# A delta-rule attention with two feed-forward layers on one core: a longer tuned order in the attention phase, and 512 columns a product in the gated layer's second part

## The chip, the core and the metric

The kernel runs on one core of a Trainium2 chip. The metric is the device time of one execution in microseconds; the times shown are medians of several runs. The profile is that of one execution, taken by the hardware profiler. TensorE (PE) multiplies matrices into PSUM, VectorE (DVE), ScalarE (ACT) and GpSimd (POOL) do the elementwise work, SyncE (SP) and ScalarE issue the transfers.

## The reference

Three layers, one after the other, all in float32 at their boundaries (the weights come as float64):

```
# attention: 4 batches, 8 heads, 768 steps, 48 dims
k_n = k / (norm(k) + 1e-06)
for t in range(S):
    y[t] = q[t] @ state
    state = state + beta[t] * outer(k_n[t], v[t] - k_n[t] @ state)
x = y as (3072 tokens, 384)
# gated layer: w_gate, w_val (384 x 1536), w_out (1536 x 384)
xn = x / sqrt(mean(x * x) + 1e-06) * rms_g
x = (silu(xn @ w_gate) * (xn @ w_val)) @ w_out
# last layer: w_in (384 x 2048), w_out (2048 x 384)
h = x @ w_in
out = (h * tanh(softplus(h))) @ w_out
```

## The kernel before

**Tiling.** The 768 steps are cut into 12 rows of 64 steps; a row holds 4 x 64 = 256 tokens (T). In the gated layer and the last layer every operand is kept as a high and a low part in float32r (names ending in h and l), and a product is three matmuls: high by high, high by low, low by high. The 1536 inner columns of the gated layer are six pairs of 256 (m); in a pair, f is one half of 128. The tiles of w_gate, w_val and w_out of pair m are `W["g", m]`, `W["v", m]` and `W["o", m]`.

**Stages.** `phase_b1` holds the attention and, between its steps, the first two pairs (FA = 2) of the gated layer for every row (`gated` with `range(FA)`): the partial sums go to `p_d` in HBM, the rows' inputs to `xh_d` and `xl_d`. `phase_b2` runs the other four pairs over all rows, loads the partial sums, adds its own, and so has the input of the last layer; `forms_of` makes the sums and differences of it that the last layer's multiplication scheme wants, splits them and stores them (`xf_d`). `phase_c` is the last layer: triples of transformed products (`triple`) with the products of w_out beside them (`down`, 384 columns). The first triple runs in `between()`, ahead of the last sums of `phase_b2`.

**Order.** All engines execute in the order in which the generators issue. In the attention phase `plan` issues the start by due times (ROW0, ROW1, QP, CV, T, G and so on), and then `merge` weaves a row's stages (listed by name in R2 to R11) with the gated layer (`part_a`), the weight conversions (`cv`) and the next segment's lanes, each by its share. In `phase_b2`, `merge` weaves the gated products (`part_b`) with the conversions, which count 192 in all.

**The second part, row by row.** For each row n and pair m, `gated` computes pg (18 matmuls of 256 columns, two halves of one PSUM tile), the silu into sg on ScalarE, pv (18 matmuls), sg times pv and the high part hh on VectorE, the low part hl on GpSimd. The down products of row n (`down`: 3 outputs x 4 pairs x 6 matmuls = 72) follow after the first pair of row n+1. Each output is then added to y (`finish_b`). Rows are loaded by `load_x` on ScalarE's queue, one row ahead, into a ring of two places (tags xh, xl). The last layer's inputs go into eight tiles `gx` and the same ring (`load_group`).

**Conversions.** `value` turns the float64 bits of 128x384 weights into float32 by one absolute value (ScalarE or VectorE) and four VectorE operations (L270, L273, L278, L281); `prepare_forms` adds and subtracts the w_in blocks (L336); `prepare_rows` does w_out of the last layer.

Of the kernel before, what the change touches and what calls it, by code (L numbers as in the profile page):

```python
# [20 lines left out]
    LN0=0.351,  # L21
    LNT=(103.075, 3.017),
    FAV=[0, 1, 1, 0, 0, 0],
    XDR=[0, 0, 0, 0, 0, 0, 1, 0, 0, 0, 0, 1],
    PDR=[0, 0, 0, 0, 0, 0, 0, 0, 0, 0, 0, 1],
    BLV=[1, 1, 0, 0, 0, 1, 0, 0, 0, 1, 1, 1],
    BAV=[0, 0, 1, 1, 1, 1, 1, 0, 0, 1, 1, 0],
    CB=[12.0, 12.0],
    PF=[5.239, 29.437, 15.946, 7.096, 7.497],
# [6 lines left out]
    LD=2.564,  # L36
# [3 lines left out]
    FP=2,  # L40
    WL=2.0,
# [8 lines left out]
    R1="r nA q0 q1 y v p o0 o1 s0 nB s1 k x0 c0 c1 g".split(),  # L50
    R2="nA r q0 Y nB q1 p y v k o0 o1 c0 c1 g".split(),
    R3="r q0 nA q1 p nB S y T X v Y k c0 o0 c1 g o1".split(),
    R4="nA q0 r T q1 p S y nB X v Y k c0 o0 c1 g o1".split(),
    R5="r nA q0 q1 p S T y nB v X Y o0 c0 k c1 o1 g".split(),
    R6="nA r q0 q1 S T y p X v Y nB k o0 c0 c1 g o1".split(),
    R7="r q0 nA q1 S p T nB v y X Y c0 o0 c1 o1 k g".split(),
    R8="r nA q0 S q1 T p y nB X v Y c1 o0 g c0 k o1".split(),
    R9="r nA q0 q1 S nB T y p X Y c1 c0 v k g o0 o1".split(),
    R10="r q0 q1 S p y X T v o0 Y k o1".split(),
    R11="S r q0 q1 p T v y X Y o0 o1 k".split(),  # L60
    DUE=[-20.443, 5.407, 4.713, 10.95, 10.883, 10.311, 10.883, 10.589, 8.191, 10.779, 10.857, 11.898],
    CVS=[0.353, 25.315, 8.774, -21.306, 9.319, -4.783, 14.063, -23.293, -15.017, -36.281, -27.539, -1.077],
    LR=[-13.795, 25.182, 18.833, 15.016, 19.193, 14.209, 19.088, 16.373, 36.251, 19.526, 57.055, 52.214],
    C={'n': 0.225, 'q': 0.5, 'r': 1.4, 'y': 1.1, 'p': 1.2, 'v': 1.2, 'o': 0.9, 'k': 1.2, 's': 0.172, 'x': 0.45, 'c':
        0.4, 'd': 0.167, 'g': 1.2, 'h': 1.228},
    ROW0=[23.019, 26.819, 30.249, 44.784, 45.626, 49.289, 33.092, 3.864, 53.626, 52.596, 54.116, 59.926, 27.667,
        37.065, 77.944],
    ROW1=[53.942, 41.233, 46.444, 57.746, 50.762, 31.696, 58.427, 60.081, 62.969, 38.184, 36.083, 63.207, 59.815,
        70.152, 81.867, 91.215, 96.339],
    QP=[[37.124, 37.533, 45.096, 22.943, 36.287], [46.104, 51.456, 18.08, 46.719, 54.368], [63.444, 60.96, 65.725,  # L70
        77.666, 71.789], [72.411, 86.727, 78.936, 75.152, 80.107]],
    L=[(19.303, 1.152), (44.964, 1.066)],
    FF=(81.946, 4.733),
    CV=[22.08, 17.591, 24.08, 74.28, 61.944, 44.711, 48.686, 65.195, 50.571, 79.022, 64.689, 83.13, 83.315, 83.796,
# [3 lines left out]
    K1=[4.777, 9.76, -11.197, -13.022],  # L78
    K23=[11.822, 14.842, 13.512, 12.77],
    K4=[45.709, 47.503, 50.123, 37.446],  # L80
    S=[-2.317, 10.764, 23.854, 22.707, 53.127],
    T=[9.259, 12.875, 27.966, 32.334],
    G=[11.277, 15.572, 4.585, 15.695],
    BL=32.701,
    CVN=13.355,
# [115 lines left out]
def kernel(  # L201
# [51 lines left out]
    def prepare(get_pool, key, cut, act=True, low=None, **kw):  # L253
        return [prepare_half(half, get_pool, key, cut, act, low or nc.gpsimd, kw) for half in range(2)]
# [238 lines left out]

    def x_tiles():
        return [xp.tile([128, KD, T], F32R, tag=tag, name=tag, bufs=XB) for tag in ("xh", "xl")]
# [7 lines left out]
    def phase_b1():  # L503
# [34 lines left out]
        bnat = xp.tile([128, KD, T], F32R, tag="xl", name="bnat", bufs=XB).bitcast(F32)  # L538
# [41 lines left out]
        def flat(t):  # L580
            return t.bitcast(F32).rearrange("p a b -> p (a b)")
# [732 lines left out]
        for m in range(FA):  # L1314
            gens.append(prepare(lambda: wa, ("o", m), rows(w_out1, m), act=not P["FAV"][4 + m], low=nc.vector))
# [18 lines left out]
        sq = [xp.tile([128, KD, T], F32R, tag="xh", name="sq", bufs=XB) for _ in range(2)]  # L1334
        sq = [flat(t)[:, 0:16 * D].rearrange("p (u d) -> p u d", d=D) for t in sq]
# [3 lines left out]
        part_a = gated((ps_u, ps_ds, hp, tp), range(FA), range(NR), get_xa, finish_a, next_x)  # L1339
# [69 lines left out]
    def phase_b2(cv, between):  # L1409
        st = ExitStack()  # L1410
        hp = st.enter_context(pool("hp2", NP1 - FA + 1, side="right"))
        tp = st.enter_context(pool("tp2", side="right"))
        ys = {}

        def next_x(n):
            if n < NR:
                load_x(n)
            if n == NR:
                load_group(0, 4)

        def finish_b(n):
            if n % 2 == 0:
                ys[n // 2] = [tpc.tile([128, 2, T], F32, tag="y", name="y", bufs=2 * KD) for _ in range(KD)]
            for o in range(KD):
                nc.scalar.dma_start(out=ys[n // 2][o][:, n % 2], in_=p_d[n][:, o, :])

            def finish(o, ps):
                y = ys[n // 2][o][:, n % 2]
                nc.vector.tensor_tensor(out=y, in0=y, in1=ps, op=ALU.add)
                if n % 2 and o == KD - 1:  # L1430
                    forming.append(forms_of(n // 2, ys.pop(n // 2)))
# [22 lines left out]
        first = [lambda g=g: load_group(0, g) for g in range(4)] + [lambda: load_raw(0)]  # L1454

        def used(n, m):
            if m == FA:
                next_x(n + 1)
            if n >= 4 and (m - FA) % 2 and first:
# [12 lines left out]
        part_b = with_forms(  # L1472
            gated((ps_u, [ps_d], hp, tp), range(FA, NP1), range(NR), lambda n: xs[n], finish_b, between=between, used=used)
        )
# [36 lines left out]
    def load_group(j, g):  # L1511
        i = (5 * j + g) % 6
        xg[j, g] = []
        for x, tag in enumerate(("xh", "xl")):
            if i < 4:
                t = w2i.tile([128, 3, T], F32R, tag="gx", name="gx", bufs=8)
            else:
                t = xp.tile([128, 3, T], F32R, tag=tag, name="gx", bufs=XB)
            nc.sync.dma_start(out=t.bitcast(F32), in_=xf_d[j][:, x, 3 * g:3 * g + 3])
            xg[j, g].append(t)  # L1520
# [48 lines left out]
    def phase_c():  # L1569
# [32 lines left out]
        def down(j, f, tt, gs):  # L1602
            if f == fs[0] and tt == 0:
                acc[:] = [ps_d.tile([128, DM], F32, tag="d", name="pd") for _ in range(4)]
# [124 lines left out]
    xs, wt, xg, forming, ring = {}, {}, {}, [], [0]  # L1729
    wbp = []  # L1730
    WE = P["WE"]
    with tc.manual_schedule():
# [3 lines left out]
        tpc = st_2.enter_context(pool("tpc", side="right"))  # L1736
        ps_u = st_2.enter_context(pool("ps_u", P["NU"], space=PSUM))
# [40 lines left out]
```

## Time and profile before

| | |
|---|---|
| median of 3 runs | 1145.95 us (1143.6 to 1147.54) |
| the profiled execution: time, span | 1142.09 us, 1140.2 us |
| mean granted TensorE clock | 0.962 |
| busy: PE, DVE, ACT, POOL | 95%, 72%, 44%, 39% of the span |

Matmuls are pipelined, so that their durations overlap: the distance from one start to the next tells what one costs in a stream, not its own duration. A clock of 1.00 is 2.4 GHz, one of 0.50 is 1.2 GHz; values between are a mean over a stretch. A line such as L419 is that of the helper that issues the matmul.

### The profile page before, as it was taken

The page shows a single profiled execution, that of the slowest core. Times are in us where ns is not written, and L with a number is a line of the kernel's source. Part 1 is how long each engine was busy: PE and PEld are TensorE (multiplying, and loading weights), DVE is VectorE, ACT ScalarE, POOL GpSimd, SP SyncE. Part 2 cuts the span into 40 slices and gives each one's busy share as a digit, 9 for nine tenths or more (in the row PEclk, how much of TensorE's full clock was granted, in tenths as well). Part 3 has the DMA queues.
Part 4 walks back from the last instruction along what each step waited for, and adds up shares of the span by engine and source line. Part 5 has one row for each costly group of instructions (what it writes and reads, how often), then busy time and mean ns, then how long its engine had stood idle before and what let it go on. Part 6 is the DMA issues. An engine that isn't in the chain of part 4 may idle for free.

```text
span 1140.2 us, 34459 instructions
## 1 busy us (share of the span) xinstructions
PE 1077.6 (95%) x14442; PEld 1041.7 (91%) x14442; DVE 822.6 (72%) x1626; ACT 500.8 (44%) x1081; POOL 447.2 (39%) x433
## 2 busy tenths in 40 slices
PE   5878699999999999999999999999999999999997
PEld 5767588989888899999999999999999999999997
DVE  7777987776878988667888994456665656565662
ACT  4576456575656732233223332224533433343333
POOL 2030343434131441466467674534533332333332
PEclk8687799999999999999999999999999999999999
DMA  9033233423126554256787887964735263452621
GB/s 170 15 77 100 71 71 74 98 77 92 53 82 186 165 188 157 95 200 233 261 299 259 268 279 251 298 230 159 241 111 193 84 210 106 141 174 79 209 64 34
DMA packets 178506, 175.34 MB, mean 154 GB/s; under 512 B 84624, under 2 KB 153232, under 8 KB 178352
## 3 DMA queue, kind: packets, MB, share of 16 engines
q1 hardware_dynamic: 169712, 159.00, 46.0%
q10 hardware_dynamic: 8640, 14.16, 3.8%
q8 instruction: 113, 1.85, 0.7%
q14 instruction: 41, 0.34, 0.1%
HBM read 114.53 MB, written 58.59 MB: 152 GB/s over the span
## 4 chain that ended last, share of the span: by engine, by line
PE 74%; DVE 15%; ACT 4%; issue 3%; DMA 2%; SPq 1%; POOL 1%; DVEq 0%; ACTq 0%; POOLq 0%
PE pd L1609 6%; PE pd L1608 6%; PE pd L1610 6%; PE ph L1651 5%; PE ph L1652 5%; PE ph L1653 5%; PE pg L419 4%; PE pd L453 4%; PE pv L419 3%; PE pd L454 3%; PE pd L455 3%; PE pg L421 3%; PE pg L420 3%; PE pv L421 3%; PE pv L420 3%
## 5 line engine op out<-in xcount | busy, mean ns | idle before, releaser
L1598 POOL TENSOR_TENSOR gl<-t,gh 128x512 fp32r<-128x512 f32 x96 | 124.1, 1294 | 246.9 <-ACT gh L1597 200.5
L1660 DVE TENSOR_TENSOR ou<-ou,ph 128x256 f32<-128x256 f32 x210 | 88.5, 421 | 118.6 <-ACT ou L1658 68.5
L481 POOL TENSOR_TENSOR hl<-sg,hh 128x512 fp32r<-128x512 f32 x72 | 102.0, 1417 | 164.5 <-DVE hh L480 150.8
L1586 ACT ACTIVATE t<-t 128x512 f32<-128x512 f32 x96 | 60.9, 634 | 184.5 <-DVE t L1660 184.3
L419 PE MATMUL pv<-xh,wvh 128*128 128x256 f32 x432 | 127.2, 294 | 1.1 <-DVE sg L477 0.8
L419 PE MATMUL pg<-xh,wgh 128*128 128x256 f32 x432 | 126.8, 293 | 0.0
L453 PE MATMUL pd<-hh,woh 128*128 128x256 f32 x420 | 121.7, 290 | 4.5 <-ACT par L1296 3.3
L421 PE MATMUL pv<-xh,wvl 128*128 128x256 f32 x432 | 123.1, 285 | 0.0
L420 PE MATMUL pv<-xl,wvh 128*128 128x256 f32 x432 | 123.1, 285 | 0.0
L420 PE MATMUL pg<-xl,wgh 128*128 128x256 f32 x432 | 123.0, 285 | 0.0
L421 PE MATMUL pg<-xh,wgl 128*128 128x256 f32 x432 | 122.8, 284 | 0.0
L454 PE MATMUL pd<-hl,woh 128*128 128x256 f32 x420 | 119.6, 285 | 2.2 <-POOL hl L481 2.2
L455 PE MATMUL pd<-hh,wol 128*128 128x256 f32 x420 | 119.2, 284 | 0.0
L1608 PE MATMUL pd<-wqh,gh 128*128 128x384 f32 x288 | 97.4, 338 | 0.0
L1609 PE MATMUL pd<-wql,gh 128*128 128x384 f32 x288 | 97.3, 338 | 0.0
L1610 PE MATMUL pd<-wqh,gl 128*128 128x384 f32 x288 | 97.1, 337 | 0.0
L471 ACT ACTIVATE sg<-pg 128x512 f32<-128x512 f32 x72 | 43.0, 598 | 122.9 <-PE pg L421 105.0
L477 DVE TENSOR_TENSOR sg<-sg,pv 128x512 f32<-128x512 f32 x72 | 49.1, 682 | 53.4 <-PE pv L421 46.4
L419 PEld LDWEIGHTS pv<-xh,wvh 128*128 128x128 f32 x432 | 83.8, 194 | 3.6 <-DVE sg L477 1.0
L453 PEld LDWEIGHTS pd<-hh,woh 128*128 128x128 f32 x420 | 80.3, 191 | 6.7 <-ACT par L1296 4.3
L419 PEld LDWEIGHTS pg<-xh,wgh 128*128 128x128 f32 x432 | 83.4, 193 | 2.3 <-issue 0.2
L420 PEld LDWEIGHTS pv<-xl,wvh 128*128 128x128 f32 x432 | 83.8, 194 | 0.0
(271 smaller groups left out, 3246.0 us busy)
## 6 DMA issues: line engine op xcount, KB each, us to landing
xf_d<-fx SPq DMA_DIRECT2D x96, 256.0 KB, 3.5
gx<-xf_d SPq DMA_DIRECT2D x60, 384.0 KB, 4.4
wr<-wi_d SPq DMA_DIRECT2D x120, 192.0 KB, 2.6
raw<-in_moe_w_out_dram SPq DMA_DIRECT2D x28, 384.0 KB, 3.9
wi_d<-ws SPq DMA_DIRECT2D x20, 384.0 KB, 3.6
raw<-in_moe_w_in_dram SPq DMA_DIRECT2D x16, 384.0 KB, 3.8
wq_d<-ws SPq DMA_DIRECT2D x16, 384.0 KB, 4.2
kh<-in_k_dram SPq DMA_DIRECT2D x24, 192.0 KB, 3.7
```

The source lines that it names most:

```text
L419: nc.tensor.matmul(ps[:, f, :], wh[:, kt, sl], xh[:, kt, :], start=(kt == 0), stop=False)
L420: nc.tensor.matmul(ps[:, f, :], wh[:, kt, sl], xl[:, kt, :], start=False, stop=False)
L421: nc.tensor.matmul(ps[:, f, :], wl[:, kt, sl], xh[:, kt, :], start=False, stop=(kt == KD - 1))
L453: nc.tensor.matmul(ps, wh[:, f, sl], hh[:, f, :], start=(i + f == 0), stop=False)
L454: nc.tensor.matmul(ps, wh[:, f, sl], hl[:, f, :], start=False, stop=False)
L455: nc.tensor.matmul(ps, wl[:, f, sl], hh[:, f, :], start=False, stop=last)
L481: nc.gpsimd.tensor_tensor(out=hl, in0=sg, in1=hh.bitcast(F32), op=ALU.subtract)
L1598: nc.gpsimd.tensor_tensor(out=gl, in0=t, in1=gh.bitcast(F32), op=ALU.subtract)
L1608: nc.tensor.matmul(ps, gh, wh, start=(f == fs[0]), stop=False)
L1609: nc.tensor.matmul(ps, gh, wl, start=False, stop=False)
L1610: nc.tensor.matmul(ps, gl, wh, start=False, stop=last)
L1660: nc.vector.tensor_tensor(out=at(to), in0=at(a), in1=at(b), op=PLUS[sign])
```

## The change

1. The constants of the attention phase's order (due times, the order of stages in rows 1 to 11, shares of the streams, which engine does a copy) have other values. The list of operations stays.
2. The gated layer's second part takes two rows at once (`gated_pairs`): one product has 512 columns (2 rows x 256), for one f of one pair. pg and pv are then 9 matmuls each. The down products of a unit (9 matmuls, into three PSUM tiles that hold the sums over all eight units of the pair of rows) are issued from a queue, `held`, that is LG = 2 units long, three at a pair of rows' first unit.
3. The places of the rows are fixed tiles: `XP` for two rows (also the ring of the attention phase), `XG[0]`, `XG[1]` and `XG[2]` = `XP`, which later hold the last layer's inputs. Row 1 is loaded after the last up product of part a (`used_a`). Partial sums are loaded at the pair FA + 2 (`load_parts`).
4. The conversions are merged with the weight 192 x PB = 230.4, and each step of `part_b` takes one step of `forms_of`.
5. beta's tile and the last w_out tile of part a share a tag (late) in pool `wa`, and the squares of two norms go into `As[1]`, since the ring is no longer tagged.

```
-    LN0=0.351,
-    LNT=(103.075, 3.017),
+    LN0=0.527,
+    LNT=(101.823, 0.05),
...
-    LD=2.564,
+    LD=2.543,
...
+    PB=1.2,
+    LG=2,
...
-    R6="nA r q0 q1 S T y p X v Y nB k o0 c0 c1 g o1".split(),
...
+    R6="nA q0 q1 S r nB T y v p X Y k o0 c0 c1 g o1".split(),
...
+    XP = xp.tile([128, 2, 2, KD, T], F32R, name="XP")
+    turns = [0]
+
     def x_tiles():
-        return [xp.tile([128, KD, T], F32R, tag=tag, name=tag, bufs=XB) for tag in ("xh", "xl")]
+        i = turns[0] % 2
+        turns[0] += 1
+        return [XP[:, x, i] for x in range(2)]
...
+        def used_a(n, m):
+            if n == NR - 1 and m == FA - 1:
+                load_x(1)
...
-        hp = st.enter_context(pool("hp2", NP1 - FA + 1, side="right"))
+        hp = st.enter_context(pool("hp2", P["LG"] + 3, side="right"))
...
+        places = [XG[(2, 0, 1)[j % 3]] for j in range(NB - 1)] + [XP]
+
+        def load_pair(j):
+            for i in range(2):
+                for x, d in enumerate((xh_d, xl_d)):
+                    nc.scalar.dma_start(out=places[j][:, x, i].bitcast(F32), in_=d[2 * j + i])
+
+        def load_parts(j):
+            while len(forming) > 1:
+                for _ in forming.pop(0):
+                    pass
+            ys[j] = [tpc.tile([128, 2, T], F32, tag="y", name="y", bufs=2 * KD) for _ in range(KD)]
             for o in range(KD):
-                nc.scalar.dma_start(out=ys[n // 2][o][:, n % 2], in_=p_d[n][:, o, :])
+                for i in range(2):
+                    nc.scalar.dma_start(out=ys[j][o][:, i], in_=p_d[2 * j + i][:, o, :])
+
+        def finish_pair(j):
 
             def finish(o, ps):
-                y = ys[n // 2][o][:, n % 2]
+                y = ys[j][o]
                 nc.vector.tensor_tensor(out=y, in0=y, in1=ps, op=ALU.add)
...
+        def gated_pairs():
+            units = [(m, f) for m in range(FA, NP1) for f in range(2)]
+
+            def up_pair(w, f, x):
+                ps = ps_u.tile([128, 2, T], F32, tag="u", name="pu")
+                wh, wl = w
+                sl = slice(f * 128, f * 128 + 128)
+                for kt in range(KD):
+                    xh, xl = (x[:, i, :, kt, :] for i in range(2))
+                    nc.tensor.matmul(ps, wh[:, kt, sl], xh, start=(kt == 0), stop=False)
+                    nc.tensor.matmul(ps, wh[:, kt, sl], xl, start=False, stop=False)
+                    nc.tensor.matmul(ps, wl[:, kt, sl], xh, start=False, stop=(kt == KD - 1))
+                return ps
+
+            def down_pair(j, m, f, hh, hl, acc, finish):
+                if not acc:
+                    acc.extend(ps_d.tile([128, 2, T], F32, tag="d", name="pd") for _ in range(KD))
+                wh, wl = W["o", m]
+                first, last = (m, f) == units[0], (m, f) == units[-1]
+                cols_of = [slice(o * 128, (o + 1) * 128) for o in range(KD)]
+                for w, h, i in ((wh, hh, 0), (wl, hh, 1), (wh, hl, 2)):
+                    for o, ps in enumerate(acc):
+                        nc.tensor.matmul(ps, w[:, f, cols_of[o]], h, start=first and i == 0, stop=last and i == 2)
+                        if last and i == 2:
+                            finish(o, ps)
+
+            held = []
+            for j in range(NB):
+                finish, acc = finish_pair(j), []
+                for m, f in units:
+                    pg = up_pair(W["g", m], f, places[j])
+                    sg = tp.tile([128, 2, T], F32, tag="sg", name="sg", bufs=2)
+                    nc.scalar.activation(out=sg, in_=pg, func=ACTF.Silu)
+                    yield 1
+                    pv = up_pair(W["v", m], f, places[j])
+                    nc.vector.tensor_tensor(out=sg, in0=sg, in1=pv, op=ALU.mult)
+                    hh = hp.tile([128, 2, T], F32R, tag="hh", name="hh")
+                    hl = hp.tile([128, 2, T], F32R, tag="hl", name="hl")
+                    nc.vector.tensor_copy(hh, sg)
+                    nc.gpsimd.tensor_tensor(out=hl, in0=sg, in1=hh.bitcast(F32), op=ALU.subtract)
+                    used(j, m, f)
+                    yield 1
+                    held.append((j, m, f, hh, hl, acc, finish))
+                    while len(held) > P["LG"] + (held[0][1:3] == units[0]):
+                        down_pair(*held.pop(0))
+                        yield 1
+            while len(held) > 1:
+                down_pair(*held.pop(0))
+            between()
+            down_pair(*held.pop(0))
...
+        def used(j, m, f):
+            if m == FA and f == 0 and j + 1 < NB:
+                load_pair(j + 1)
+            if (m, f) == (FA + 2, 0):
+                load_parts(j)
+            if 3 <= j < NB - 1 and f and first:
                 first.pop(0)()
-            if n == NR - 1:
-                for _ in range(4):
-                    todo.pop(0)()
+            if j == NB - 1:
+                if m == FA:
+                    load_group(0, f)
+                if m == NP1 - 1 and f:
+                    load_group(0, 4)
+                if f:
+                    for _ in range(4):
+                        todo.pop(0)()
 
         def with_forms(part):
-            for i, w in enumerate(part):
+            for w in part:
                 yield w
-                turn = i % 3 < 2 if len(ys) == 0 else i % 2
-                if forming and turn and next(forming[0], 0) is not None:
+                if forming and next(forming[0], 0) is not None:
                     forming.pop(0)
...
-        total = NR * 4 * nb + (NR - 1) * 6 - 4 * nb
-        merge((budget(part_b, total), total), (cv, P["CVB1"]))
+        part_b = with_forms(gated_pairs())
+        total = NB * 8 * 3 - P["LG"]
+        merge((budget(part_b, total), total), (cv, P["CVB1"] * P["PB"]))
```

## Rows read from the trace of the kernel before

**Rows 1.** The page, busy time, share and count by engine.
```profile
PE 1077.6 (95%) x14442; PEld 1041.7 (91%) x14442; DVE 822.6 (72%) x1626; ACT 500.8 (44%) x1081; POOL 447.2 (39%) x433
```
**Rows 2.** Windows over the span: each engine's busy time (count), clock, DMA.
```profile
0.00:50.00 50.00, 33.38 (x872) 30.52 (x872) 39.91 (x97) 24.41 (x44) 8.43 (x22) 0.80 0.58 99
...
100.00:150.00 50.00, 36.64 (x870) 33.66 (x864) 45.97 (x97) 27.57 (x56) 10.72 (x10) 0.75 0.36 98
...
600.00:650.00 50.00, 50.00 (x420) 50.00 (x419) 46.00 (x69) 17.85 (x42) 35.67 (x33) 1.00 0.81 268
```
**Rows 3.** Waits of PE, 0 to 150 us: us in total, times, longest.
```profile
PE pp L782 <- issue: 7.5, 1, 7.5
...
PE pp L762 <- ACT QT L783: 5.0, 2, 2.8
```
**Rows 4.** Timeline of PE: the second part's first product, and the first behind it.
```profile
434.03 0.28 PE L419 MATMUL pg<-xh,wgh 128*128 128x256 f32 x1
...
759.30 0.28 PE L1651 MATMUL ph<-gx,wi 128*128 128x256 f32 x1
```
**Rows 5.** Timeline of PE, first and last of 864 products in a stretch.
```profile
461.22 0.28 PE L455 MATMUL pd<-hh,wol 128*128 128x256 f32 x1
...
564.74 0.36 PE L454 MATMUL pd<-hl,woh 128*128 128x256 f32 x1
```
**Rows 6.** Timeline of PE in the last layer, first and last of 323 products.
```profile
896.75 0.34 PE L1609 MATMUL pd<-wql,gh 128*128 128x384 f32 x1
...
943.07 0.34 PE L1610 MATMUL pd<-wqh,gl 128*128 128x384 f32 x1
```
**Rows 7.** Timeline of PE: products that waited, with idle time before and releaser.
```profile
459.65 0.39 PE L453 MATMUL pd<-hh,woh 128*128 128x256 f32 x1 [0.95 <-DVE hh L480]
461.00 0.39 PE L454 MATMUL pd<-hl,woh 128*128 128x256 f32 x1 [0.96 <-POOL hl L481]
...
668.75 0.39 PE L453 MATMUL pd<-hh,woh 128*128 128x256 f32 x1 [0.25 <-DVE hh L480]
670.34 0.39 PE L454 MATMUL pd<-hl,woh 128*128 128x256 f32 x1 [1.21 <-POOL hl L481]
```
**Rows 8.** Windows behind the second stall, columns as in rows 2.
```profile
671.50:675.00 3.50, 3.50 (x19) 3.50 (x18) 3.43 (x5) 0.86 (x3) 3.50 (x4) 0.53 0.96 286
675.00:679.00 4.00, 4.00 (x35) 4.00 (x34) 3.97 (x6) 1.58 (x4) 3.75 (x5) 1.00 0.94 342
```
**Rows 9.** Windows of the second part by kind of conversion, columns as in rows 2.
```profile
436.00:628.00 192.00, 189.76 (x1575) 189.01 (x1575) 153.53 (x286) 58.83 (x137) 106.11 (x104) 1.00 0.66 221
628.00:703.00 75.00, 73.54 (x598) 73.13 (x597) 64.86 (x97) 24.21 (x55) 49.05 (x45) 0.98 0.84 276
703.00:744.00 41.00, 41.00 (x344) 41.00 (x343) 15.75 (x27) 9.65 (x22) 19.21 (x21) 1.00 0.84 278
```
**Rows 10.** Groups of DVE instructions, 432 to 706 us: busy us, mean ns, idle before.
```profile
L281 DVE SCALAR_TENSOR_TENSOR t<-raw,t 128x384 int32<-128x384 int32 x37 | 34.5, 933 | 1.3
L477 DVE TENSOR_TENSOR sg<-sg,pv 128x512 f32<-128x512 f32 x41 | 27.9, 681 | 25.6 <-PE pv L421 21.6 <-POOL ws L321 2.9 <-ACT sg L471 1.0
...
L480 DVE CAST hh<-sg 128x512 fp32r<-128x512 f32 x41 | 23.2, 567 | 1.4
```
**Rows 11.** Timeline of DVE: one conversion operation, twice.
```profile
449.53 0.56 DVE L281 SCALAR_TENSOR_TENSOR t<-raw,t 128x384 int32<-128x384 int32 x1
...
452.31 1.53 DVE L281 SCALAR_TENSOR_TENSOR t<-raw,t 128x384 int32<-128x384 int32 x1
```
**Rows 12.** Timeline of POOL beside the second of them.
```profile
451.89 1.54 POOL L481 TENSOR_TENSOR hl<-sg,hh 128x512 fp32r<-128x512 f32 x1 [3.20 <-DVE hh L480]
```
**Rows 13.** DMA issues: count, size, median us from issue to landing.
```profile
xl<-xl_d ACTq DMA_DIRECT2D x12, 384.0 KB, 5.7
```
**Rows 14.** Timeline of DVE, the end of the first triple's sums.
```profile
751.69 0.74 DVE L1660 TENSOR_TENSOR t<-t,ph 128x256 f32<-128x256 f32 x2
```

More of the change, by code (lines that the diff above doesn't have):

```diff
@@ L58 @@
[L58 to L65, printed above, removed]
@@ new lines @@
+    R5="r nA q0 q1 p S T y nB X v Y o0 c0 k c1 o1 g".split(),
+    R6="nA q0 q1 S r nB T y v p X Y k o0 c0 c1 g o1".split(),
+    R7="r q0 nA q1 S p nB T v y X Y c0 o0 c1 o1 k g".split(),
+    R8="r nA q0 S T q1 p X y nB v Y c1 o0 g c0 k o1".split(),
+    R9="r nA q0 S q1 nB T p X c1 y v k g Y c0 o0 o1".split(),
+    R10="r q0 q1 p S y X T v o0 Y o1 k".split(),
+    R11="S r q0 q1 p T y X Y v o0 k o1".split(),
+    DUE=[-20.443, 5.84, 4.881, 10.56, 10.883, 10.311, 10.883, 10.566, 8.191, 10.779, 10.857, 11.898],
@@ new lines @@
+    CVS=[-0.332, 18.493, 8.167, -23.236, 9.058, -3.972, 15.147, -22.515, -14.058, -35.503, -28.424, -8.878],
+    LR=[-10.2, 25.182, 19.094, 12.02, 16.416, 13.382, 22.451, 16.703, 20.252, 19.685, 56.75, 78.665],
+    C={'n': 0.225, 'q': 0.5, 'r': 1.4, 'y': 1.1, 'p': 1.2, 'v': 1.2, 'o': 0.9, 'k': 1.38, 's': 0.168, 'x': 0.595,
+        'c': 0.4, 'd': 0.167, 'g': 1.02, 'h': 1.357},
+    ROW0=[23.019, 25.696, 30.249, 44.915, 45.626, 49.289, 21.158, 3.409, 52.039, 52.631, 54.162, 59.926, 14.374,
+        44.933, 77.944],
@@ new lines @@
+    ROW1=[53.942, 35.537, 46.444, 56.274, 50.209, 32.154, 23.865, 62.891, 61.444, 37.535, 36.083, 60.421, 59.815,
+        70.152, 81.857, 92.68, 97.453],
+    QP=[[37.124, 37.533, 39.845, 25.37, 23.991], [46.104, 51.456, 11.475, 45.951, 54.368], [63.368, 60.96, 66.42,
+        77.445, 60.154], [72.13, 86.727, 76.657, 67.584, 71.475]],
+    L=[(19.303, 1.152), (44.964, 1.232)],
+    FF=(82.023, 4.733),
+    CV=[25.704, 17.591, 24.08, 74.28, 62.288, 44.711, 48.686, 65.143, 48.122, 77.711, 64.689, 82.826, 83.011,
[3 rows of a table added]
@@ L81 @@
+    K1=[-14.887, 8.58, -15.344, -13.163],
+    K23=[12.298, 15.952, 13.512, 12.77],
+    K4=[45.709, 47.503, 50.123, 37.537],
     S=[-2.317, 10.764, 23.854, 22.707, 53.127],
[L82 to L85, printed above, removed]
+    T=[8.74, 12.356, 29.899, 32.334],
+    G=[11.07, 18.231, 4.585, -15.646],
+    BL=33.889,
+    CVN=12.886,
 )
@@ L537, in phase_b1 @@
         even, odd, top = (qc[:, 192 + i:193 + i] for i in range(3))
-        bnat = xp.tile([128, KD, T], F32R, tag="xl", name="bnat", bufs=XB).bitcast(F32)
+        bnat = wa.tile([128, KD, T], F32, tag="late", name="bnat", bufs=2)
         bnat = bnat.rearrange("p a b -> p (a b)")[0:32, 0:S]
@@ L1314, in phase_b1 @@
         for m in range(FA):
-            gens.append(prepare(lambda: wa, ("o", m), rows(w_out1, m), act=not P["FAV"][4 + m], low=nc.vector))
+            kw = dict(tag="late", bufs=2) if m == FA - 1 else {}
+            gens.append(prepare(lambda: wa, ("o", m), rows(w_out1, m), act=not P["FAV"][4 + m], low=nc.vector, **kw))
         cv = convs(gens, 3)
@@ L1333, in phase_b1 @@
         spare = rp.tile([128, 16, 64], F32, tag="PT", name="spare")[:, :, 0:D]
-        sq = [xp.tile([128, KD, T], F32R, tag="xh", name="sq", bufs=XB) for _ in range(2)]
-        sq = [flat(t)[:, 0:16 * D].rearrange("p (u d) -> p u d", d=D) for t in sq]
+        sq = [As[1].rearrange("p a b -> p (a b)")[:, i * 768:i * 768 + 768] for i in range(2)]
+        sq = [t.rearrange("p (u d) -> p u d", d=D) for t in sq]
         sq.append(ch.tile([128, 16, D], F32, tag="sq", name="sq"))
@@ L1338, in phase_b1 @@
         ps_ds = [ps_d]
-        part_a = gated((ps_u, ps_ds, hp, tp), range(FA), range(NR), get_xa, finish_a, next_x)
+        def used_a(n, m):
+            if n == NR - 1 and m == FA - 1:
+                load_x(1)
+        part_a = gated((ps_u, ps_ds, hp, tp), range(FA), range(NR), get_xa, finish_a, next_x, used=used_a)
         def turned(r):
@@ L1452, in phase_b2 @@
         todo += [lambda x=x: load_q(2, x, in_wb) for x in "hl"]
[L1454 to L1459, printed above, removed]
-                first.pop(0)()
-            if n == NR - 1:
-                for _ in range(4):
-                    todo.pop(0)()
+        first = [lambda: load_group(0, 2), lambda: load_group(0, 3), lambda: load_raw(0)]
+        def used(j, m, f):
[4 more added lines that the diff above has]
+            if 3 <= j < NB - 1 and f and first:
+                first.pop(0)()
+            if j == NB - 1:
[6 more added lines that the diff above has]
+                        todo.pop(0)()
         def with_forms(part):
-            for i, w in enumerate(part):
+            for w in part:
                 yield w
-                turn = i % 3 < 2 if len(ys) == 0 else i % 2
-                if forming and turn and next(forming[0], 0) is not None:
+                if forming and next(forming[0], 0) is not None:
                     forming.pop(0)
-        part_b = with_forms(
-            gated((ps_u, [ps_d], hp, tp), range(FA, NP1), range(NR), lambda n: xs[n], finish_b, between=between, used=used)
-        )
-        total = NR * 4 * nb + (NR - 1) * 6 - 4 * nb
-        merge((budget(part_b, total), total), (cv, P["CVB1"]))
+        part_b = with_forms(gated_pairs())
+        total = NB * 8 * 3 - P["LG"]
+        merge((budget(part_b, total), total), (cv, P["CVB1"] * P["PB"]))
         for _ in cv:
@@ L1513, in load_group @@
         xg[j, g] = []
[L1514 to L1518, printed above, removed]
+        for x in range(2):
+            t = XG[i // 2][:, x, i % 2]
             nc.sync.dma_start(out=t.bitcast(F32), in_=xf_d[j][:, x, 3 * g:3 * g + 3])
@@ L1603, in down @@
             if f == fs[0] and tt == 0:
-                acc[:] = [ps_d.tile([128, DM], F32, tag="d", name="pd") for _ in range(4)]
+                acc[:] = [ps_d.tile([128, 512], F32, tag="d", name="pd")[:, :DM] for _ in range(4)]
             gh, gl = (g[:, tt * 128:tt * 128 + 128] for g in gs)
@@ L1727, in phase_c @@
         st.close()
-    xs, wt, xg, forming, ring = {}, {}, {}, [], [0]
+    xs, wt, xg, forming, ring, XG = {}, {}, {}, [], [0], []
     wbp = []
@@ L1736 @@
         tpc = st_2.enter_context(pool("tpc", side="right"))
+        XG.extend(w2i.tile([128, 2, 2, KD, T], F32R, name=f"XG{i}") for i in range(2))
+        XG.append(XP)
         ps_u = st_2.enter_context(pool("ps_u", P["NU"], space=PSUM))
```

45 lines of the change are left out of this document (11 added, 34 removed), and 6 rows, old and new, of the table CV.

## The prediction

> **What bounds the kernel now.** I read the page's busy times first, then the table of windows over the whole span, then the timeline of TensorE in the gated layer's second part, then the waits of the other engines there. TensorE is busy for 1077.6 of 1140.2 us, VectorE for 822.6 [rows 1]; but a busy TensorE only means that products overlap, so the start-to-start spacing counts. The windows tell three regimes apart [rows 2]: in the first 150 us of the attention phase TensorE has gaps and a mean clock of 0.75 to 0.80; from 150 us on it is full at a clock near 1.00, and VectorE at 46.0 of 50 us (600 to 650 us) is nearly full beside it. The gated layer's second part (four of six pairs of weights, all 12 rows) runs from its first up product at 434.03 us to the first product of the last layer's second triple at 759.30 us [rows 4]: 325.27 us for 12 x 4 x 54 = 2592 products of 256 columns and the 45 of the last layer's first triple, which is put in ahead of the last sums.
>
> In a steady stretch the products start at 461.22 and 564.74 us with 863 intervals between them, so one takes 103.52 / 863 = 0.11995 us [rows 5]. At that spacing 2637 products make 316.3 us; 9.0 us of the 325.27 are lost. The stalls that I can see are two pairs of waits of the down products for VectorE's hh and GpSimd's hl, 0.95 + 0.96 us at 460 and 0.25 + 1.21 us at 669 [rows 7]; after the second the granted clock falls to 0.53 for some 3.5 us, in which 19 products run where 35 run in the next 4.0 us [rows 8], a loss of some (3.5 - 19 x 0.12) = 1.2 us. So this part is bound by TensorE's stream, with VectorE close behind.
>
> **The products of 512 columns.** 2592 products become 1296. Weight loads and products halve in number, columns stay. No 512-column product stands in the trace, so I bound it. 256 columns take 119.95 ns, which is 106.7 ns at 2.4 GHz and 13.3 more. In the last layer 180 products of 256 and 142 of 384 columns lie between the starts at 896.75 and 943.07 us [rows 6]: (46.32 - 180 x 0.11995) / 142 = 174.1 ns for 384 columns, 160.0 and 14.1 more. The extra is thus nearly the same for both, a price per product, not per column. The line through both points (54.2 ns for 128 columns) gives 228.3 ns at 512; a constant extra gives 226.6. The dear end is twice the 256-column time, 239.9 ns (no gain); the cheap end is no extra at all, 213.3 ns. I take 228.3, since two rows lie on that line: 1296 x (239.9 - 228.3) = 15.0 us saved; the ends give 0 and 34.5 us.
> The Trainium skill (TensorE: Matmul & The Clock Gate, Back-to-back issue gap) puts a warm product at N/2.4 plus 2.5 ns, so 109.2 ns at 256 columns; the trace's 119.95 disagrees. By the page 512 columns would take 215.8 ns and the change would save 31 us; this is the first rival below.
>
> **The stalls before, and what is late next.** Now the down products of a pair follow a row later: the last hh and hl of a row are needed 36 up products (4.3 us) after their own. After the change each unit (18 products up, one f of one pair) gives its h to a queue that is two units long (three at the start of a pair of rows): 2 x 27 products x 0.2283 = 12.3 us. The silu, product, copy and subtraction keep their size (128x512) and their number (48 each); the sums into y become 18 of 512 columns in place of 36 of 256. So the visible stalls should go: 3.4 us of waits and 1.2 of clock; the rest of the 9.0 (some 2.1 of it in the triple, which is unchanged) I leave.
> Against it stands the pace of the weight conversions. They are merged into the products by weights: 192 before, which is about their true sum (188 by the code's yields), so that they ended at 87% of the part; the windows show VectorE at 64.9 of 75 us from 628 to 703 and at 15.75 of 41 from there on [rows 9]. The new 1.2 x 192 = 230 lets them end at 72%. Count VectorE's demand until then: 153.5 + 64.9 = 218.4 us before [rows 9], of which 41 units' products and copies are 27.9 + 23.2 = 51.1 [rows 10]; the other 167.3 must now fit, with 0.72 x 48 = 34.6 units x 1.25 us = 43.2, into 0.72 x 301 = 217 us (301 = 295.9 of products and 5.4 of the triple): 210.5, or 97%. In the dense stretch (the 16 half blocks of w_out2, 628 to 703 us before, now 58.7 us): 64.9 - 11.4 x 1.25 = 50.6, plus 9.5 x 1.25 = 11.9, makes 62.5 in 58.7 us, so VectorE falls 3.8 us behind. The queue of two units covers that (12.3 less the 2.4 us of mult, copy and subtraction), but not if VectorE starts the stretch behind.
> How much slower VectorE gets in company is seen at one line: L281 takes 0.56 us at 449.53 and 1.53 us at 452.31 [rows 11], where GpSimd's subtraction of 451.89 to 453.43 runs [rows 12]; its mean is 0.933 us [rows 10].
> The Trainium skill (SBUF — State Buffer, Who interferes with whom) calls the read port that the two engines share an exclusive lock, and the trace agrees with it here. It speaks against denser conversions: more of them meet GpSimd.
> From the rows: L281 alone has 37 x (0.933 - 0.56) = 13.8 us of such inflation; if the four conversion operations together have two to three times that and it grows by a tenth, VectorE's demand reaches 214 of 217 us. I take 4 us of new stalls and clock loss for it (estimate; below it 0, above it the third rival).
>
> **The two ends of the part.** The first product now needs rows 0 and 1. Row 1 goes to the place that row 11 of part a has just read, so its load starts after the last up product of that row; 36 down products (some 5 us before 434.03) cover it. Such a load lands after 5.7 us in the median under heavier traffic [rows 13]: a wait of 0.5 us, between 0 and 5. At the other end the last sums after the first triple shrink from 72 products of 256 (8.6 us) to 9 of 512 (2.1 us). VectorE ends the triple's sums at 752.4 us [rows 14], 1.8 us after TensorE, so 2.1 us still covers it; GpSimd's first splits for the last layer lie bare, and I take 1 us (0 to 3). The group of transformed inputs that goes into the rows' own place (the fifth) is loaded after the last up product, with two sets of sums and 36 products (8.4 us) ahead of its use: nothing, unless the queue on SyncE is behind. The other moves (tiles held as fixed places, the square scratch in As[1], beta's tile with w_out's) issue the same instructions.
>
> **The attention phase.** Its constants change: orders of a few stages in ten rows swap neighbours, due times move by a few units. No operation is added. TensorE's idle time there is mostly in the first 150 us: 16.6 us in the first 50, 13.4 between 100 and 150 [rows 2], the largest being 7.5 us of issue and 5.0 for a transposed q [rows 3]. A shuffle can win or lose parts of this; I take 0, with 6 us to either side, about one such wait.
>
> **Sum.** -15.0 (products) - 4.6 (stalls) + 0.5 + 4 + 1 + 0 = -14.1 us. The profiled execution's own time, 1142.09 us, becomes 1128.0; the median of the runs shown, 1145.95, lies 3.9 us above it, so 1132.
>
> **Rivals.**
> (1) The extra per product is hidden at 512 columns: in the cold stretch products start every 0.21 us, about 256 / 1.2 GHz, with no extra to be seen, so something that takes a fixed time may lie beside a long enough product. Against it: 384 columns show 14.1 ns. Products 31 to 34.5 us cheaper instead of 15: 1113 to 1116.
> (2) The extra grows with the columns (512 take 239.9 ns), so the change does nothing to the products: -14.1 + 15.0 = +0.9: about 1147, no difference. For it: 14.1 against 13.3 ns is a rise; against it: it should have been 20 ns.
> (3) The other side: VectorE becomes the bound while the conversions last. It decides once VectorE's demand passes 217 + 9.9 us (the queue's cover), 8% above my 210.5; to eat the gain it must be 217 + 9.9 + 4 + 14.1 = 245, 16% above it; at 20% (253 us) the part stalls 26 us in place of 4 and the kernel takes 1154 us. For it: VectorE was at 92% from 600 to 650 us already [rows 2], and the stall at 669 was its own; against it: most of its load is the same work, only earlier, and the queue is longer.
> (4) The order of the attention phase loses more than one of the idle waits seen (over 14 us) and takes all the gain: from 1146 upward. For it speaks only that the rows there are tightly chained.
>
> **Chances.** The forecast 0.66 (1120 to 1142); (1) 0.11, (2) 0.09, (3) 0.09, (4) 0.05. A difference of 0.3%, 3.4 us, is about what a measurement of this kernel can tell from none. Faster takes all of (1) and 0.64 of the forecast, and 0.03 of (2) through the attention phase: 0.78. Slower: (3) 0.07 of its 0.09, (4) 0.03, (2) 0.02: 0.12. Same: 0.10. The range leaves out the cheap tip of (1) and the dear half of (3) and (4): 1114 to 1147.
>
> **What the profile would show.** Steady starts every 0.228 us in the second part, 1296 products there, and its length near 311 us; VectorE above 95% up to about 72% of the part and then nearly idle; waits of down products for hl gone at its start; at most 1 us ahead of its first product. Wrong: spacing of 0.240 or 0.216 us; rows of waits for sg, hh or hl with a clock below 1.00 between 55% and 75% of the part; the attention phase, now 434 us to the first product, longer or shorter by more than 6 us.

## The result, and the profile after

The changed kernel takes 1130.82 us (median of 4 runs, 1128.78 to 1133.71) beside 1146.18 for the kernel before on the same chips: 0.987 of it, 95% interval 0.9839 to 0.9902. The profiled execution went from a span of 1140.2 us to 1127.5. The forecast of 1132 us holds to about 1 us, but three of its terms are off and cancel, as the profile shows.

The page's busy times, which answer to [rows 1]: 1296 matmuls fewer, TensorE's busy time 13 us less, VectorE's nearly the same.

```profile
PE 1064.6 (94%) x13146; PEld 970.4 (86%) x13146; DVE 826.8 (73%) x1609; ACT 498.8 (44%) x1076; POOL 451.1 (40%) x435
```

The same windows as in [rows 2]:

```profile
0.00:50.00 50.00, 32.02 (x754) 29.08 (x756) 37.47 (x94) 21.05 (x39) 6.22 (x19) 0.79 0.59 98
...
100.00:150.00 50.00, 35.64 (x929) 33.26 (x923) 43.83 (x97) 26.51 (x51) 9.60 (x10) 0.77 0.31 91
...
600.00:650.00 50.00, 45.95 (x194) 35.60 (x193) 48.90 (x67) 17.61 (x41) 34.84 (x32) 1.00 0.88 293
```

From 600 to 650 us VectorE is now at 48.9 of 50 us and TensorE, which was full there, waits for 4 us. The timeline of TensorE at the two ends of the second part, beside [rows 4]:

```profile
427.89 0.47 PE L1461 MATMUL pu<-XP,wgh 128*128 128x512 f32 x1
428.93 0.47 PE L1462 MATMUL pu<-XP,wgh 128*128 128x512 f32 x1 [0.56 <-DMA XP<-xl_d]
...
746.51 0.28 PE L1720 MATMUL ph<-XG,wi 128*128 128x256 f32 x1
```

The 12.7 us of the span split in three. The attention phase ends 6.1 us earlier (427.89 for 434.03). The second part, last sums and first triple included, takes 318.6 us in place of 325.3, 6.7 less. The last layer is unchanged (381.0 and 380.9 us from there to the end). In the second part, the starts of one unit (18 up and 9 down products) and the next, first for rows read from XP, then from XG[0]:

```profile
458.09 0.40 PE L1461 MATMUL pu<-XP,wgh 128*128 128x512 f32 x1
...
464.32 0.40 PE L1461 MATMUL pu<-XP,wgh 128*128 128x512 f32 x1
...
501.99 0.39 PE L1461 MATMUL pu<-XG,wgh 128*128 128x512 f32 x1
...
508.29 0.39 PE L1461 MATMUL pu<-XG,wgh 128*128 128x512 f32 x1
```

A unit that waits for nothing takes 6.23 us in one place and 6.30 in the other, all along the part; a product thus 0.2307 or 0.2333 us. With three pairs of rows (24 units) in each kind of place the products make 24 x (6.23 + 6.30) = 300.7 us, 10.2 below the 310.9 of before. Of the 318.6 us, 5.4 are the triple's products and 12.5 are lost (9.0 before). TensorE's waits in the part, beside the 0.56 us above (us, times, longest):

```profile
PE pu L1461 <- DVE sg L1487: 3.5, 4, 1.5
PE pu L1461 <- ACT sg L1484: 2.5, 2, 1.9
```

No down product of the part waits any more. Of these waits 1.3 and 0.6 us lie at the part's start (440 and 445 us), the others between 623 and 650. Two windows of the part, one of the kernel before, and the stretch behind the longest wait, columns as in [rows 2]:

```profile
427.89:618.00 190.11, 187.64 (x807) 151.14 (x807) 164.72 (x286) 61.53 (x143) 110.27 (x104) 1.00 0.65 220
618.00:656.00 38.00, 33.95 (x135) 25.70 (x134) 37.07 (x54) 12.58 (x30) 22.20 (x21) 0.96 0.83 277
```
```profile
628.00:688.00 60.00, 58.54 (x473) 58.13 (x472) 58.48 (x89) 22.20 (x51) 40.81 (x38) 0.97 0.82 267
```
```profile
649.50:654.00 4.50, 4.45 (x13) 3.50 (x14) 4.40 (x8) 0.00 (x0) 1.42 (x2) 0.62 0.93 351
```

VectorE's last conversion operation starts at 660.4 us, 73% of the part. From 618 to 656 us VectorE is busy for 37.07 of 38 us, TensorE waits, and after the longest wait the granted clock falls to 0.62 for 4.5 us. That wait is put down to ScalarE's silu, but the silu (648.92 us) stands behind a copy of ScalarE that had waited for VectorE's conversion:

```profile
648.05 0.51 ACT L357 CAST ws<-t 128x384 fp32r<-128x384 f32 x1 [3.02 <-DVE t L283]
```

In the kernel before, VectorE's last conversion operation starts at 687.7 us, at 78% of its part and not 87%, and from 628 to 688 us it was as full already (58.48 of 60 us); the window to 703 us of [rows 9] holds 15 us more in which VectorE converts nothing.

### The profile page after: what moved, and what is told of

It is laid out like the page before. It is cut to its first block, busy times and chain, and to the rows that moved or that the text cites. A ratio compares the mean times of both kernels' runs of the same rounds, so it can differ in the third digit from the quotient of the medians.

```text
span 1127.5 us, 31819 instructions
## 1 busy us (share of the span) xinstructions
PE 1064.6 (94%) x13146; PEld 970.4 (86%) x13146; DVE 826.8 (73%) x1609; ACT 498.8 (44%) x1076; POOL 451.1 (40%) x435
## 4 chain that ended last, share of the span: by engine, by line
PE 79%; DVE 10%; ACT 5%; issue 3%; DMA 2%; SPq 1%; POOL 0%; ACTq 0%; POOLq 0%; DVEq 0%
PE pd L1474 7%; PE pd L1679 6%; PE pd L1678 6%; PE pd L1677 6%; PE ph L1720 5%; PE ph L1721 5%; PE ph L1722 5%; PE pu L1461 4%; PE pu L1463 4%; PE pu L1462 4%; PE pp L769 2%; PE pp L1023 2%; PE pg L421 2%; PE pd L455 2%; PE pp L1181 2%
## 5 line engine op out<-in xcount | busy, mean ns | idle before, releaser
L283 DVE SCALAR_TENSOR_TENSOR t<-raw,t 128x384 int32<-128x384 int32 x68 | 60.6, 892 | 2.4
L1666 ACT CAST gh<-t 128x512 fp32r<-128x512 f32 x96 | 59.5, 621 | 3.9
L1562 POOL TENSOR_TENSOR fx<-xu,fx 128x256 fp32r<-128x256 f32 x60 | 49.9, 839 | 17.4 <-ACT fx L1561 16.4
L1677 PEld LDWEIGHTS pd<-wqh,gh 128*128 128x128 f32 x288 | 54.5, 189 | 0.0
L1678 PEld LDWEIGHTS pd<-wql,gh 128*128 128x128 f32 x288 | 54.4, 189 | 0.0
L1679 PEld LDWEIGHTS pd<-wqh,gl 128*128 128x128 f32 x288 | 54.0, 188 | 0.4 <-POOL gl L1667 0.4
L280 DVE SCALAR_TENSOR_TENSOR t<-raw,t 128x384 int32<-128x384 int32 x68 | 46.6, 685 | 1.4
L421 PE MATMUL pg<-XP,wgh 128*128 128x256 f32 x144 | 45.5, 316 | 0.0
L421 PE MATMUL pv<-XP,wvh 128*128 128x256 f32 x144 | 44.9, 312 | 0.0
L275 DVE TENSOR_SCALAR t<-t 128x384 int32<-128x384 int32 x68 | 42.7, 627 | 2.3
L455 PE MATMUL pd<-hh,woh 128*128 128x256 f32 x132 | 39.8, 301 | 2.3 <-ACT par L1303 2.2
```

The source lines that it names most:

```text
L283: nc.vector.scalar_tensor_tensor(out=ti, in0=low, scalar=29, in1=ti, op0=ALU.logical_shift_right, op1=ALU.bitwise_or)
L421: nc.tensor.matmul(ps[:, f, :], wh[:, kt, sl], xh[:, kt, :], start=(kt == 0), stop=False)
L455: nc.tensor.matmul(ps, wh[:, f, sl], hh[:, f, :], start=(i + f == 0), stop=False)
L1666: nc.scalar.copy(gh, t)
L1677: nc.tensor.matmul(ps, gh, wh, start=(f == fs[0]), stop=False)
L1678: nc.tensor.matmul(ps, gh, wl, start=False, stop=False)
```

## Experiments

All ratios are to the kernel before, run on the same chip in turn with the experiment, with 95% intervals.

**What is the order worth, and what the new second part?** The changed kernel with the old constants, and the kernel before with the new ones:

```
 e1: P = dict(... as before ..., PB=1.2, LG=2)     # rest as changed
 e2: P = dict(... as changed ...)                  # rest as before
```

> The changed kernel with the constants of the attention phase's order from before. Theory A (both halves of the change gain: the profile of the changed kernel reaches the second part's first product at 427.9 us in place of 434.0, and the second part is 6.7 us shorter): about 1137 us, the first product at 434 us again. Theory B (the order is worth nothing, as the prediction took it; the 6 us are chance or come with the new start of the second part): about 1131 us, within 2 us of the changed kernel.

> The kernel before with the new constants of the order and nothing else. Theory A: about 1140 us, 6 below the kernel before, the second part as long as before (325 us). Theory B: 1146 us, no difference.

The old order with the new part is at 0.9906 (0.9885 to 0.9927), the new order with the old part at 0.994 (0.992 to 0.9959): 10.8 and 6.9 us. Both halves gain, and their sum (17.7 us) meets the change's 14.9 within the intervals. The profiles agree: the second part begins at 436.65 us with the old order in the new kernel, at 429.64 with the new order in the old one, and takes 315.6 and 324.9 us. Theory A holds, though the old order in the new kernel is faster than its 1137 us (1133.57). Its part is 3 us shorter than the changed kernel's with much the same waits: the first product doesn't wait for row 1, and after the same wait of 1.9 us for a silu the granted clock stays at 1.00 there.

**Is it the width of the products?** Each product of 512 columns issued as two of 256, all else as changed:

```
-  nc.tensor.matmul(ps, wh[:, kt, sl], xh, ...)
+  for n in range(2):   # the rows' halves one after the other
+      nc.tensor.matmul(ps[:, n, :], wh[:, kt, sl], x[:, 0, n, kt, :], ...)
```

> The changed kernel with each product of 512 columns issued as two of 256 (same units, queue and pace). If the width of the products pays, as the trace says (0.2315 us on average in place of 2 x 0.120): 1296 x 0.0085 = 11 us slower, less some 3 us of stalls that a slower stream no longer meets: 1138 to 1142 us. By the forecast's line (0.2283): 1144 to 1146. Rival (the width is worth nothing; pairs of rows, the queue and the longer lead of loads make the gain): 1131 us.

0.9944 (0.9924 to 0.9963), 1137.53 us: what the new order alone gives. The part takes 325.7 us, as before the change. So pairs of rows, the queue and the new pace are worth nothing to be seen without the width; with it the part gains some 7 us. Each product comes with its own weight load [rows 1], so the run doesn't separate what a product costs from what its weight load costs.

**Are the new waits VectorE's demand?** First the pace of the conversions, PB 1.2 to 1.0:

> The changed kernel with the conversions merged at 192 in place of 230. If the denser conversions cost the waits between 623 and 654 us (4 us of idle time and some 2 us at the lower clock), they shrink and the time falls to 1125 to 1128 us. Rival 1 (the same VectorE work only moves, the waits with it): 1131. Rival 2 (the early pace is needed for the loads of the last layer's weights): slower, 1133 to 1136.

0.9907 (0.9888 to 0.9926), 1133.63 us; the part takes 320.8 us, 2.2 longer. The waits for VectorE's sg fall from 3.5 to 0.4 us, but another wait is born, in the list of TensorE's waits and on ScalarE's timeline:

```profile
PE ph L1720 <- ACT sg L1484: 4.1, 1, 4.1
```
```profile
740.23 0.40 ACT L1561 CAST fx<-xu 128x256 fp32r<-128x256 f32 x1 [6.92 <-DMA xf_d<-fx]
740.54 0.59 ACT L1484 ACTIVATE sg<-pu 128x512 f32<-128x512 f32 x1
```

A silu stands behind a copy that waits for a tile whose store is queued on SyncE among the loads of the last layer's weights, and the triple's bank waits for the silu. Rival 2 fits: the quick pace brings these loads forward. The ratio's interval meets that of the changed kernel, so this rests on the trace. Then the same load spread otherwise:

```
-    WK=2.0,  PB=1.2,
+    WK=1.0,  PB=1.07,
```

> The changed kernel with the steps of the transformed weights counted lighter (2.0 to 1.0 each) and the whole at 1.07 in place of 1.2, so that these are issued closer together and the blocks of the last layer's w_out further apart, while all end at about the same place. If the waits at 623 to 654 us are VectorE's demand in that dense stretch (waits for sg, and the clock behind them, 6 to 7 us): they shrink to 0 to 3 us, the second part takes 313 to 316 us in place of 318.6, and the kernel is 0.984 of the kernel before. Rival (VectorE's total demand before the conversions end is what counts): the waits move to the front, the time stays at 0.987.

1.0013 (1.0 to 1.0026): all of the gain is gone, and neither theory had foreseen the size. The part takes 331.2 us. The waits are not smaller but spread:

```profile
PE pu L1461 <- DVE sg L1487: 8.2, 5, 3.0
PE pu L1461 <- ACT sg L1484: 6.5, 4, 3.2
```

Counting the w_in blocks lighter issued them closer together, and these had no room either. Which of the engines behind them (VectorE's sums, ScalarE's copies, GpSimd's splits) set that, the run doesn't separate. So VectorE was relieved without moving anything in time:

```
-                    nc.vector.tensor_copy(hh, sg)
+                    nc.scalar.copy(hh, sg)
```

> The changed kernel with the high part hh of the second part's units copied on ScalarE and not on VectorE: 48 copies of some 0.57 us leave VectorE (27 us in 319). If VectorE's busy time is the bound at 618 to 656 us, its waits fall and the second part is 3 to 5 us shorter. Rival (ScalarE runs in order, so the next silu stands behind a copy that waits for VectorE's product): waits for ScalarE take their place, the same time or up to 10 us longer.

0.9851 (0.9836 to 0.9867), which meets the interval of the changed kernel; in the profile the part takes 315.9 us, 2.7 less. The same 38 us as above:

```profile
618.00:656.00 38.00, 36.91 (x158) 29.20 (x157) 34.23 (x49) 17.26 (x39) 24.27 (x23) 1.00 0.89 302
```

VectorE is off its limit, TensorE runs 158 products there in place of 135 at a clock of 1.00, and ScalarE, the rival, has room. These 23 products are some 5 us; part of it is lost again at the part's start, where TensorE waits 1.95 us for ScalarE's silu (0.59 in the changed kernel) and the clock falls behind it. Whether the copies on ScalarE cause that is not shown: the run at the pace of 192, with hh on VectorE, has 2.08 us there. Last, the queue (LG 2 to 1):

> The changed kernel with the queue of the down products one unit long. If the queue's length is what lets TensorE run on while VectorE is behind (12.3 us of cover at two units, 6.2 at one), waits of down products for hh and hl come back in the dense stretch and at the start: 3 to 8 us longer than the changed kernel. Rival (the cover is set by the four PSUM tiles of the up products, where the changed kernel waits already): no difference beyond 1 us.

0.9941 (0.9927 to 0.9954), the part 324.4 us, 5.8 longer, with the wait that the queue of two had removed:

```profile
PE pd L1474 <- DVE hh L1490: 8.8, 7, 3.0
```

**Why is a product dearer than 0.2283 us?** First the two runs of 256 addresses laid side by side:

```
-  XP = xp.tile([128, 2, 2, KD, T], F32R, name="XP")
+  XP = xp.tile([128, 2, KD, 2, T], F32R, name="XP")   # XG alike
```

> The changed kernel with the two rows of a place laid side by side, so that the 512 columns of an up product are one run of addresses and not two of 256. The spacing of up products is 0.229 us from XP and 0.233 us from XG. If the break between the two runs costs the extra, both fall to 0.2266 (a constant extra of 13.3 ns) or less and the second part is 3 to 6 us shorter. Rival (the extra has nothing to do with the run of addresses; down products have one run and take 0.234): no change of the spacing, the time within 2 us of the changed kernel, or longer by the smaller runs of the loads.

0.9881 (0.9862 to 0.9899); a unit takes 6.23 us from XP and 6.30 from XG, as in the changed kernel: the break costs nothing. What does tell the places apart is the compiled program's addresses: XP and the gated weights start at multiples of 64 bytes, all tiles of the pools on the right side (XG, hh, hl, y, the last layer's inputs) at 32 above one. So these were shifted. The weights of the second part start at multiples of 64 with and without the shift, so in its products from XG and its down products only the operand that brings the columns moves:

```
+    shift = ctx.enter_context(pool("shift", side="right")).tile([128, 8], F32, name="shift")
+    nc.vector.memset(shift, 0.0)
```

> The changed kernel with one more tile of 32 bytes at the end of SBUF, so that every tile of the pools on the right side (XG, the h tiles, y, the last layer's inputs and first weights) starts 32 bytes lower: at a multiple of 64 bytes, as XP and the gated weights do already, and not 32 above one. If the price of a product hangs on where its operands start (0.2267 us for pv from XP, 0.231 for pg from XP, 0.2333 from XG, 0.234 for down products with h tiles): all products of the second part fall to about 0.227 us, 1296 x 0.0045 = 6 us shorter, and the last layer may gain too: 1118 to 1125 us, 0.977 to 0.983 of the kernel before. Rival (the extra hangs on something else, such as which PSUM bank or which engines run beside): the same spacing by tile, the same time as the changed kernel, 0.987.

0.9823 (0.9796 to 0.985), 1122.78 us; the interval just meets that of the changed kernel, so the reading rests on the spacing. A unit from XG:

```profile
504.77 0.39 PE L1463 MATMUL pu<-XG,wgh 128*128 128x512 f32 x1
...
510.95 0.39 PE L1463 MATMUL pu<-XG,wgh 128*128 128x512 f32 x1
```

6.18 us, 0.2289 a product, up and down, and not the 0.227 that was expected. From XP a unit takes 6.21: its down products fell too, its up products, whose operands stayed where they were, did not (0.2318 for pg and 0.2271 for pv, 0.2309 and 0.2267 without the shift). On average a product takes 0.2294 in place of 0.2320. The part takes 315.2 us (3.5 less, with 1.9 us more waits for VectorE's sg than before the shift), the last layer 2.7 less. Only this one shift was run; that it is the start within 64 bytes that counts, and not some other effect of the place, is argued from the addresses. And the kernel before with the same shift:

> The kernel before with the same shift by 32 bytes and nothing else. If the start of the operands costs something for every product, whatever its width: in the changed kernel the shift took 2.7 us from the last layer (256 columns 0.1193 to 0.1174 us) and should do so here, and 2 to 5 us more in the second part if its products fall from 0.11995 as well: 0.992 to 0.996 of the kernel before. Rival (only products of 512 columns are hit in the second part, so that the missing gain belongs to the change): the spacing there stays at 0.11995 and the kernel is at 0.997 to 0.998.

0.9916 (0.9896 to 0.9937). The first and last of 846 products in a stretch, to be read beside [rows 5]:

```profile
465.67 0.29 PE L457 MATMUL pd<-hh,wol 128*128 128x256 f32 x1
...
566.52 0.39 PE L456 MATMUL pd<-hl,woh 128*128 128x256 f32 x1
```

100.85 / 845 = 0.11935 us in place of 0.11995: the price of the start is paid by 256 columns too. The down products alone, whose h tiles moved, fell from 0.1200 to 0.1178, the up products stayed. That is half of the 4.4 ns that 512 columns gain from XG. The part is 1.6 us shorter, the last layer 3.0, the attention phase 0.8 longer. The ratio says 9.6 us. The two profiles are single executions: that of the shifted kernel (1138.44 us) lies 2.4 above its median, that of the kernel before (1142.09) 2.2 below the median it is compared with here (1144.32), which would make up most of the difference.

**Which part of the order gains?** The due times of rows 0 and 1 from before, the rows' orders and shares as changed:

> The changed kernel with the due times of the attention's start (rows 0 and 1, the first segments' lanes) from before, and the new orders and shares of rows 2 to 11. The changed kernel's start is 3 us later than before (row 0's state update at 60.2 us in place of 57.1, row 1's at 85.4 in place of 82.7), its rows 2 to 11 gain 9 us. If the gain is in the rows' orders and the new start costs: the first product of the second part at 424 to 426 us, the kernel at 1127 to 1129. Rival (the later start is what lets the rows run without waits): at 428 or later, the kernel at 1131 to 1134.

0.9852 (0.9833 to 0.9871); the second part begins at 425.8 us. In the eight other profiles with the new order and without the shift it begins between 427.9 and 431.1. The gain comes after 150 us: from there to 424 us TensorE runs more products in the changed kernel (first line) than in the kernel before (second), and as many in this run (5967).

```profile
150.00:424.00 274.00, 268.11 (x5968) 249.64 (x5965) 230.45 (x379) 173.23 (x413) 105.55 (x105) 1.00 0.41 114
150.00:424.00 274.00, 264.25 (x5822) 244.53 (x5821) 221.83 (x357) 171.89 (x411) 100.97 (x102) 0.98 0.39 108
```

So the gain is in the rows. That the new start costs is not shown: the ratio's interval meets that of the changed kernel, and the two runs with the shift in the changed kernel, whose attention phase is the same, begin the second part at 424.9 and 429.4 us, with a granted clock of 0.74 and 0.69 in their first 150 us.

**Both remedies together.** The shift, and hh on ScalarE:

> The shift by 32 bytes and the high part hh on ScalarE together: the version that should beat both kernels. If the two effects are separate (one per product, one in VectorE's dense stretch) they add: 1115 to 1122 us, 0.975 to 0.981 of the kernel before, the second part 307 to 311 us. Rival (faster products only run into VectorE's demand sooner): no better than the better of the two alone, 0.985.

0.9785 (0.9763 to 0.9808), 1119.58 us: below both kernels, with the part at 311.9 us, just above the range. They add: of the 11 us against the changed kernel, 6.7 are in the part (3.5 and 2.7 alone) and 2.4 in the last layer.

## Why the prediction was right, and where it was not

- **Products, -15.0 forecast, -10.2 measured.** That the width gives the part's gain is right (the run with 256 columns). The term is mis-sized: 0.2320 us on average in place of 0.2283. The step that failed is the price of 384 columns. It was worked out with 0.11995 us for the 180 products of 256 columns in [rows 6], a spacing read in the gated layer. In that stretch of the last layer itself, averaged over the runs of three or six like products, 256 columns take 0.1192 us and 384 take 0.1751, so the extras are 12.5 and 15.1 ns and not nearly the same; the line through these two gives 0.2310 at 512, close to what was measured, and -11.5 us. That the line is a rule is not shown: over the whole last layer the line gives 0.2317 without the shift (0.1193 and 0.1755 us) and 0.2334 with it (0.1174 and 0.1754), while 512 columns fell to 0.2294. The Trainium skill (TensorE: Matmul & The Clock Gate, Back-to-back issue gap) has a formula that gives an estimate of 215.8 ns; the cheapest products here, pv from XP, take 226.7, so rival 1 is out. The products did get cheaper than twice 256 columns, so rival 2 is out too.
- **Stalls, from 9.0 to 9.9 forecast, 12.5 measured.** The waits of the down products went as forecast, and the run with a queue of one brings them back. The next thing late was named rightly: VectorE in the dense stretch. Its 97% held there (37.07 of 38 us) and not all the way to 72% of the part: up to 656 us VectorE is busy for 201.8 of 228.1 us, where the forecast had 210.5 of 217. The stretch was read too wide ([rows 9] up to 703 us), so that its own fullness, 58.5 of 60 us before the change already, didn't show. The 4 us put down for it came out near 7 (0.5 + 1.6 + 0.5 + 2.1 of longer spacing at four waits; the rest, 2.3, in the products behind them, seven of which start 0.43 us apart at the lower clock). The cover of 12.3 us was counted for the down products; what ran out was the up products' tiles, which wait for sg. The same waits cost 2.4 us at the part's start, where the forecast had none left. Rival 3 is this mechanism; it did not reach its point.
- **The ends of the part.** The first product waited 0.56 us for row 1 (0.5 forecast). The passage to the last layer cost nothing to be seen: triple and last sums take 9.8 us from 736.70 to 746.51.
- **The attention phase, 0 forecast, about -6 measured.** This step failed: "A shuffle can win or lose parts of this; I take 0". The 6.1 us lie at the edge of the bound given (6 us), and they are not in the idle time of the first 150 us, where I looked: that is longer now (18.0 and 14.4 us in the two windows, for 16.6 and 13.4). They are won after 150 us, where TensorE looked full: its idle time from there to the second part was 10.3 us and is 6.4, its granted clock 0.98 and is 1.00, and the run with the old start and the new rows has the gain as well. The starts of the second part scatter by some 4 us between profiles, but the three with the old order (434.0, 434.8 and 436.7 us) lie above all ten with the whole new order (424.9 to 431.1).
- **The sum** held because 4.8 us too much for the products and 2.6 too little for the stalls were made up by the 6.1 of the order. That is luck: nothing ties the gain of the order to the other two.
- **The forecast's own signs of being wrong.** Two came true though the time hit: waits for sg with a clock below 1.00 (0.62) between 55% and 75% of the part, and an attention phase changed by more than 6 us.

## What to carry to other kernels

A price per instruction can be read from two widths in the same trace and drawn to a third, as an estimate; take both prices from the same stretch, and check that the new width's operands start where those of the rows did. When a stream gets faster, find the engine beside it that is nearly full (VectorE here), read that in windows no wider than its dense stretch, and count which buffer runs out first, for every consumer: the longer queue covered the down products, not the up products. And a sum that hits is not yet a right sum: the split by stages (where the part begins, how long it takes, what follows) showed in three numbers that one term stood in for another.

## What the runs showed of the hardware that was not expected

Moving tiles by 32 bytes changes what a float32r product takes in a stream. With the operand that brings the columns at 32 above a multiple of 64 bytes, 512 columns take 0.2333 us (from XG and in the down products), with it at a multiple 0.2289; for 256 columns it is 0.1200 and 0.1178 (down products of the second part in the kernel before). A tile of 32 bytes gives the kernel before 0.8% and the changed one some 0.5%. The start is not all: up products from XP, at a multiple of 64 in every run, take 0.2267 for pv and 0.2309 for pg without the shift; what sets these apart is not settled. Nor is a wait always followed by a lower clock: behind the same wait of 1.9 us the granted clock fell to 0.62 in the changed kernel and stayed at 1.00 with the old order.
